# Single-bank PSUM tiles, a third row maximum in two half-width parts, and exponentials per 512 columns in a two-layer FNet and attention kernel

## The chip, the cores and the metric

The kernel runs on one core of a Trainium2 chip. A core has a matrix engine (TensorE, in the profile PE for matmuls and PEld for the loading of weights), a vector engine (DVE), a scalar engine (ACT), GpSimd (POOL) and a queue that issues most transfers (SP). Matmuls write to PSUM, a memory of eight banks of 512 float32 columns by 128 partitions; DVE and ACT read it. The metric is the device time in microseconds of one execution, and the median of several runs is reported.

## The reference, cut to what matters

```python
x = A_x                                            # 2048 x 512, float32
x = x + A(layernorm(x))                            # FNet
x = x + B(layernorm(x))                            # attention
x = x + A(layernorm(x))
x = x + B(layernorm(x))

def A(x):
    a = einsum("bsd,ed->bse", x, dft_hid_re)
    b = einsum("bsd,ed->bse", x, dft_hid_im)
    return einsum("ts,bse->bte", dft_seq_re, a) - einsum("ts,bse->bte", dft_seq_im, b)

def B(x):                                          # S = 2048, D = 512, 32 heads of 16
    q = (x @ wq).reshape(B, S, 32, 16).transpose(0, 2, 1, 3)
    k, v = x @ wk, x @ wv                          # one key and value head for all 32
    scores = einsum("bhqd,bkd->bhqk", q, k) * 16 ** -0.5
    o = einsum("bhqk,bkd->bhqd", softmax(scores), v)
    return o.transpose(0, 2, 1, 3).reshape(B, S, 512) @ wo
```

The softmax needs, for each of 2048 queries and 32 heads, the maximum of 2048 scores before the exponentials.

## The kernel before

Each of the two layers has a phase A (the FNet part, the layer normalisations, and the making of queries, keys and values) and a phase B (attention). The order of all instructions on each engine is written out by hand; the framework puts in the waits.

**PSUM.** The eight banks are given out under three names. `x` has two tiles of two banks each (`pair`, L68), `y` has three single banks and `z` one (`bank`, L65). A tile of a name is reused in turn, and a new use waits until the last reader of the whole tile is done. In phase A, `x` holds the sums of the sequence transform (`z_rows`, L854; two pairs make four accumulators) and of other products (`y_rows`, L632; `q_half`, L354; `q_rows`, L363). In phase B it holds the scores.

**Queries and keys.** A query tile `i` is 128 queries; there are NT = 16 of them per layer. `o.qT[i]` holds its 32 heads as 16 pairs `pr`; of a pair, one head lies in partitions 0 to 63 and one in 64 to 127 (`g` is 0 or 1). Queries and keys are split into high and low parts, which lie in 64 rows together, so a score matmul is 64 rows deep and occupies one row half of the matrix engine; two matmuls of different `g` can run side by side. `kz` holds the keys for both halves.

**The attention loop** (`phase_b`, L1213) runs over 16 x 32 steps, n = 32 i + s_. A step scores one block `c` of 128 keys against half of the heads of tile `i`: four matmuls `score` (L1031, matmul at L1048) of 512 columns, j = 0 to 3, with g = j mod 2. Two of them, one per row half, fill the two banks of an `x` tile, and one exponential of 1024 columns on ACT reads both (L1051) into a probabilities tile `ptiles` in `slot`. Two steps later `pv` (L1055, matmuls at L1062) multiplies the probabilities with the values: four matmuls, written as eight in the profile, 128 rows deep and 32 columns wide side by side, into the one bank of `z`. After 16 key blocks ACT and DVE copy the sum out (L1065, L1068).

**The maxima** for later query tiles are made in the same steps. A piece is 512 keys `kb` of one head: `max_half` (L555) calls `max_of` (L431), a matmul of 64 rows and 512 columns into a `y` bank (L434) and a `reduce_max` on DVE (L435) into the column `kb` of `o.mxp[i]`. `units` (L1000) lists all pieces of a layer in order, `more_max` takes the next one, and `share` (L1018) says whether a step makes two or three. The order in a step is score g, score 1-g, two maxima (one per half), score 2+g, score 3-g, third maximum. With three in a step the third stands alone, and the next step begins with the other half. When a tile's pieces are done, `max_neg_a` (L571) reduces its columns, and two steps later the negated maxima go by DMA into spare rows of `o.qT` (`max_rows`, L585), so that the score matmul subtracts them.

**Once per tile** the output of the tile before is projected at step 13 (`o_proj`, L1123, twelve full matmuls into a `y` bank, then an addition on DVE, L1129), and small statistics run on DVE for the next layer's normalisation (L1174 to L1189). In the last tile, when no maxima are left, the second score pair of a step uses two `y` banks and two exponentials of 512 columns (L1039 to L1044).

Of the kernel before, what the change touches and what calls it, by code (L numbers as in the profile page):

```python
# [17 lines left out]
P = 128  # L18
# [30 lines left out]
def fnet_mqa_kernel(ctx: ExitStack, tc: tile.TileContext, x_in, ct, dt_, wq, wkv, wo, out):  # L49
# [49 lines left out]
    eps = sb.tile([P, 1], F32, name="eps")  # L99
    nc.gpsimd.memset(eps, EPS)  # L100
    kone = sb.tile([P, 1], F32, name="kone")
    kmask = sb.tile([P, 1], F32, name="kmask")
    t_ = sb.tile([P, 1], F32, name="ktmp")
# [90 lines left out]

    class Layer:
        pass

    def make_layer(L, src, mid, dst, last):
# [4 lines left out]
        o.mxp = {}  # L203
        o.qT = {}
# [149 lines left out]
        def q_half(t0, g, xth, xtl, between=lambda: None):  # L354
            wh, wl = st["wqh", g]
            pq = pair()[:, 0, :256]
            for k in range(NK):
                ks = slice(k * P, (k + 1) * P)
                mm3(pq, wh[:, ks], wl[:, ks], xth[:, k, :], xtl[:, k, :], k == 0, k == NK - 1)
                between()  # L360
            q_split(t0, g, pq)

        def q_rows(t0, g0, xth, xtl, after):  # L363
            pq = pair()
            for h in range(2):
                for k in range(NK)[::1 - 2 * h]:
                    ks = slice(k * P, (k + 1) * P)
                    for u in (0, 1, 2)[::1 - 2 * h]:
                        for g in range(2):
# [3 lines left out]
                            nc.tensor.matmul(pq[:, g ^ h, :256], a[gs, ks], b[gs, k, :],  # L373
# [4 lines left out]
            for e in range(2):  # L378
                q_split(t0, g0 + e, pq[:, e, :256])
# [51 lines left out]
        def max_of(i, pr, g, c0, n, to, tag="y"):  # L431
            pm = bank(tag)[:, :n]
            gs = slice(64 * g, 64 * g + KR)
            nc.tensor.matmul(pm, o.qT[i][gs, pr, :], kz[gs, c0:c0 + n], start=True, stop=True)  # L434
            nc.vector.reduce_max(to, pm, axis=AX.X)  # L435

# [130 lines left out]
        def max_neg(i, p0=0, n=NPAIR, k=4):  # L567
# [3 lines left out]
        def max_neg_a(i, p0=0, n=NPAIR, k=4):  # L571
# [60 lines left out]
        def y_rows(tb, pairs, zh, zl, x1, after):  # L632
            ys = [pair() for _ in pairs]
            at = 0
            for h in range(2):
                for w, y in zip(pairs, ys):
                    for cc, k in [(c, k) for c in range(2) for k in range(NK)][::1 - 2 * h]:
                        for u in (0, 1, 2)[::1 - 2 * h]:
                            a, b = ((zh, dh), (zh, dl), (zl, dh))[u]
                            for g in order(0, 1):  # L640
                                gs = slice(64 * g, 64 * g + 64)
                                tt = w[g ^ h]
                                nc.tensor.matmul(y[:, g ^ h, :], a[cc][gs, k, tt * P:(tt + 1) * P], b[cc][gs, k, :],  # L643
# [8 lines left out]
                    else:  # L652
                        for e in range(2):
                            y_add(4 * tb + w[e], y[:, e, :], x1[w[e]])
# [128 lines left out]
        def phase_a(extra):  # L783
# [125 lines left out]
            for n in range(128):  # L909
# [7 lines left out]
                if s == 0:  # L917
                    za, zb = pair(), pair()
                    z = [za[:, 0, :], za[:, 1, :], zb[:, 0, :], zb[:, 1, :]]
# [69 lines left out]
            def rows_in():  # L989
# [10 lines left out]
        units = [(0, pr, g, 3) for pr in range(HALF, NPAIR) for g in range(2)]  # L1000
        units += [(i, pr, g, kb) for i in range(1, NT) for pr in range(NPAIR) for kb in range(4) for g in range(2)
                  if (i, pr, kb) not in early]
        o.done = 0

        def more_max():
            if o.done < len(units) and units[o.done][0] in o.loaded | {0}:
                max_half(*units[o.done])
                o.done += 1

        goals = []  # L1010
        for j in range(NT):
            for lim in (HALF, NPAIR):
# [3 lines left out]
                goals.append((sum(u[0] < j or (u[0] == j and u[1] < lim) for u in units), at))  # L1016

        def share(n):  # L1018
            slack = min([3 * (at - n) - (c - o.done) for c, at in goals if at > n], default=99)
            if slack >= SPARE:  # L1020
                st["light"] = True
            elif slack < 1:
                st["light"] = False
            return 2 if st.get("light") and n >= 4 else 3

        def done_with(i, pr):
            return all(u[:2] > (i, pr) for u in units[o.done:])
# [3 lines left out]
        def score(i, s_, j):  # L1031
# [6 lines left out]
            w = j // 2  # L1038
            if i == NT - 1 and jj == 1 and o.done == len(units):  # L1039
                e = bank("y")  # L1040
                nc.tensor.matmul(e, kz[64 * g:64 * g + KR, c * P:(c + 1) * P],  # L1041
                                 o.qT[i][64 * g:64 * g + KR, cp:cp + 4, :], start=True, stop=True)
                nc.scalar.activation(ptiles[i, s_][:, j, :], e, AF.Exp, scale=DH ** -0.5)
                return  # L1044
            first = "e" not in st
            if first:
                st["e"] = pair()
            nc.tensor.matmul(st["e"][:, g, :], kz[64 * g:64 * g + KR, c * P:(c + 1) * P],  # L1048
                             o.qT[i][64 * g:64 * g + KR, cp:cp + 4, :], start=True, stop=True)
            if not first:  # L1050
                nc.scalar.activation(ptiles[i, s_][:, 2 * w:2 * w + 2, :], st.pop("e"), AF.Exp, scale=DH ** -0.5)  # L1051
# [62 lines left out]
        def o_mm(k):  # L1114
            if k == 0:
                bt["po"] = bank("y")
# [11 lines left out]
        def o_add(i):  # L1128
            nc.vector.tensor_add(bt["x"], bt["po"], bt["x"])  # L1129
            (nc.sync if last else nc.gpsimd).dma_start(dst[i], bt["x"])  # L1130

        def finish():
# [3 lines left out]
            pt = bank("y")  # L1136
# [5 lines left out]
            rc = sb.tile([P, 4, 4], F32, name="rc")  # L1142
# [7 lines left out]
            pt = bank("y")[:, :256]  # L1150
# [62 lines left out]
        def phase_b(nxt):  # L1213
            nonlocal woh, wol, osp
            woh = slot(4, F32R).rearrange("p (k e) -> p k e", k=NK)
# [6 lines left out]
            for n in range(NT * NSTEP):  # L1222
# [48 lines left out]
            for at in behind:  # L1271
                pv(*at)
            return {**out_tasks(NT - 1), 12: [lambda: o_proj(NT - 1)]}
# [65 lines left out]
```

## Time and profile before

| What | us |
|---|---|
| median of 3 runs | 3532.45 |
| lowest and highest run | 3527.42, 3532.56 |
| span of the profiled execution | 3530.1 |
| PE, DVE, ACT, POOL busy in it | 3490.8, 2606.6, 2548.1, 877.0 |

The profile describes one execution, and its span is 2.35 us below the median of the runs. A row of the grouped view gives the line, the engine, the operation, output and input tiles and shapes, the count, then the busy time, the mean in ns of one, and the idle time of the engine before it with what ended that. A row of the timeline gives start and length in us from the start of the span, the engine, the line, the operation, how many of one kind are merged, and in brackets the idle time before it and what ended it. A row of the windows view gives a stretch, its length, the busy time and count of PE, PEld, DVE, ACT and POOL in it, the granted clock of the matrix engine, the share of the transfer engines and GB/s. PE's busy time counts a matmul from its start to its modelled end, and these overlap, so a busy share near 1 doesn't by itself say that PE is the limit.

### The profile page before, as it was taken

To read this page: it belongs to the slowest core of one execution; us is meant where nothing else is said; L and a number is where in the kernel's file an instruction comes from. 1 tells how busy PE (TensorE), PEld (TensorE's weight loads), DVE (VectorE), ACT (ScalarE), POOL (GpSimd) and SP (SyncE) were. 2 spreads that over 40 slices of the span, in tenths; PEclk is the share of its full clock that TensorE was granted. 3 is DMA by queue.
4 is the path that set the end of the run, shared out by engine and by line. 5 is a ranking of instruction groups with operands and counts; after the bars stand their busy time and mean duration, and the time that the engine had idled before them with its cause. 6 is when DMAs were issued, how large, how long until landed. Compare 5 with 4: busy or idle time off the path is not lost.

```text
span 3530.1 us, 64709 instructions
## 1 busy us (share of the span) xinstructions
PE 3490.8 (99%) x24576; PEld 1874.1 (53%) x24576; DVE 2606.6 (74%) x4903; ACT 2548.1 (72%) x3324; POOL 877.0 (25%) x1342
## 2 busy tenths in 40 slices
PE   8999999999999999999999999999999999999999
PEld 6887979433333333333378879883333333333333
DVE  6264756788888888888432747668888888888883
ACT  4325644888888888888932256549888888888888
POOL 4245452211221122112213454422101010111011
PEclk9999999999999999999999999999999999999999
DMA  6435242311111110111144352423111111011100
GB/s 189 151 143 185 85 156 85 91 50 35 36 39 48 32 26 23 50 35 26 40 138 124 127 160 103 140 70 93 44 35 35 50 35 38 23 35 38 37 24 25
DMA packets 225530, 255.62 MB, mean 72 GB/s; under 512 B 52896, under 2 KB 175040, under 8 KB 218052
## 3 DMA queue, kind: packets, MB, share of 16 engines
q1 hardware_dynamic: 210932, 234.04, 21.7%
q0 software_dynamic: 14144, 17.33, 1.6%
q8 instruction: 193, 3.16, 0.4%
q14 instruction: 117, 0.96, 0.1%
q10 hardware_dynamic: 144, 0.13, 0.0%
HBM read 187.69 MB, written 65.79 MB: 72 GB/s over the span
## 4 chain that ended last, share of the span: by engine, by line
PE 90%; issue 3%; POOL 2%; DVE 2%; ACT 2%; DMA 1%; SPq 0%; ACTq 0%; DVEq 0%; POOLq 0%
PE z L1062 29%; PE x L1048 19%; PE y L434 13%; PE x L863 10%; PE y L88 3%; PE y L89 3%; PE y L90 2%; PE y L523 2%; PE x L88 2%; PE x L90 2%; PE x L89 2%; PE z L523 1%; PE x L643 0%; DVE row L193 0%; PE y L1041 0%
## 5 line engine op out<-in xcount | busy, mean ns | idle before, releaser
L1051 ACT ACTIVATE slot<-x 128x1024 f32<-128x1024 f32 x2000 | 1946.5, 1025 | 276.7 <-PE x L1048 271.6
L435 DVE TENSOR_REDUCE mxp<-y 128x1 f32<-128x512 f32 x2912 | 1830.8, 684 | 190.7 <-PE y L434 178.2
L1062 PE MATMUL z<-slot,v 128*32 128x512 f32 x8192 | 1096.3, 605 | 1.6 <-DVE lnv L1186 0.7
L1048 PE MATMUL x<-slot,kz 64*128 64x512 f32 x2976 | 676.5, 450 | 1.9 <-ACT slot L1051 0.9
L1048 PEld LDWEIGHTS x<-slot,kz 64*128 64x128 f32 x2976 | 278.3, 183 | 746.0 <-ACT slot L1051 689.4
L434 PE MATMUL y<-kz,slot 64*128 64x512 f32 x2144 | 568.3, 395 | 0.4 <-DVE mxp L435 0.4
L1062 PEld LDWEIGHTS z<-slot,v 128*32 128x32 f32 x8192 | 163.4, 108 | 360.8 <-issue 329.7
L863 PE MATMUL x<-cl,xnh 64*128 64x512 f32 (+1 forms) x1536 | 352.1, 355 | 0.0
L863 PE MATMUL x<-ch,xnh 64*128 64x512 f32 (+1 forms) x1536 | 334.8, 359 | 7.1 <-ACT row L850 7.0
L863 PE MATMUL x<-ch,xnl 64*128 64x512 f32 (+1 forms) x1536 | 338.7, 359 | 0.2 <-ACT xnl L630 0.2
L434 PEld LDWEIGHTS y<-kz,slot 64*128 64x128 f32 x2144 | 270.7, 186 | 20.7 <-DVE mxp L435 8.2
L593 POOL DMA_DIRECT2D slot<-mt x224 | 111.7, 506 | 574.6 <-PE y L434 523.3
L1105 POOL TENSOR_TENSOR row<-row,row 128x256 f32<-128x256 f32 x63 | 47.1, 747 | 707.2 <-DMA row<-rd 683.7
L863 PEld LDWEIGHTS x<-ch,xnh 64*128 64x128 f32 x1536 | 202.9, 186 | 28.9 <-ACT row L850 9.6
L863 PEld LDWEIGHTS x<-cl,xnh 64*128 64x128 f32 x1536 | 210.9, 186 | 13.8
L863 PEld LDWEIGHTS x<-ch,xnl 64*128 64x128 f32 x1536 | 204.4, 186 | 20.8 <-issue 6.0
L79 ACT CAST ch<-craw 128x512 fp32r<-128x512 f32 x176 | 106.9, 627 | 125.3 <-PE x L90 87.1
L523 PE MATMUL y<-kz,slot 64*128 64x512 f32 x496 | 194.8, 400 | 0.4
L88 PE MATMUL x<-ch,xnh 128*128 128x512 f32 x384 | 154.2, 402 | 9.3 <-ACT ch L79 8.4
L80 POOL TENSOR_TENSOR cl<-craw,ch 128x512 fp32r<-128x512 f32 x96 | 122.2, 1294 | 135.2 <-ACT ch L79 118.0
L90 PE MATMUL x<-ch,xnl 128*128 128x512 f32 x384 | 153.1, 399 | 2.6 <-POOL xnl L709 2.6
L89 PE MATMUL x<-cl,xnh 128*128 128x512 f32 x384 | 152.7, 398 | 0.6 <-DVE cl L80 0.6
(216 smaller groups left out, 4474.5 us busy)
## 6 DMA issues: line engine op xcount, KB each, us to landing
craw<-ct_in SPq DMA_DIRECT2D x112, 512.0 KB
slot<-qd SPq DMA_DIRECT2D x44, 1024.0 KB
qd<-row SPq DMA_DIRECT2D x144, 128.0 KB
od<-row SPq DMA_DIRECT2D x252, 64.0 KB
row<-wqd SPq DMA_DIRECT2D x48, 256.0 KB
row<-x_in SPq DMA_DIRECT2D x32, 256.0 KB
mid<-row POOLq DMA_DIRECT2D x32, 256.0 KB, 2.4
craw<-ct_in SPq DMA_DIRECT2D x32, 256.0 KB
```

The costliest lines, as they stand in the source:

```text
L80: (eng or nc.vector).tensor_sub(lo, raw, f(hi))
L88: nc.tensor.matmul(ps_, ah, bh, start=start, stop=False)
L89: nc.tensor.matmul(ps_, ah, bl, start=False, stop=False)
L90: nc.tensor.matmul(ps_, al, bh, start=False, stop=stop)
L434: nc.tensor.matmul(pm, o.qT[i][gs, pr, :], kz[gs, c0:c0 + n], start=True, stop=True)
L435: nc.vector.reduce_max(to, pm, axis=AX.X)
L523: nc.tensor.matmul(pm, o.qT[i][gs, pr, :], k[gs, c0:c0 + 512], start=True, stop=True)
L593: (nc.gpsimd if r else nc.sync).dma_start(f(o.qT[i][row:row + 1, p0:p0 + n, 32 * a:32 * a + 32]), mt[32 * a + c:32 * a + c + n, 32 * b:32 ...
L863: nc.tensor.matmul(z[d], a[gs, s, d * P:(d + 1) * P], b[gs, :], start=first and q < 2 and e == 0, stop=last and q > 1 and e == len(turns) - 1)
L1048: nc.tensor.matmul(st["e"][:, g, :], kz[64 * g:64 * g + KR, c * P:(c + 1) * P], o.qT[i][64 * g:64 * g + KR, cp:cp + 4, :], start=True, sto ...
L1051: nc.scalar.activation(ptiles[i, s_][:, 2 * w:2 * w + 2, :], st.pop("e"), AF.Exp, scale=DH ** -0.5)
L1062: nc.tensor.matmul(a[32 * j:32 * j + 32, :], v1[:, c, :], pt[:, j, :], start=c == 0, stop=c == NT - 1)
```

## The change

All PSUM tiles become single banks: `x` has four, and `pair` gives a list of two. In phase B the banks are taken once per layer and passed round by hand: `o.x`, four for the scores, and `o.banks`, three for maxima, projection and the last tile. Each score has its own exponential of 512 columns. A step with three maxima makes two whole ones and, as the third, a part: 256 keys of one head in one row half and the same 256 keys of its partner in the other, side by side in one bank. One reduce gives both maxima. Between the two matmuls of a part, DVE copies one element from the first one's columns into the second one's, which makes the second wait for the first. The partial maxima have six columns for four: whole pieces use `kb`, parts use `kb` and `kb + 2` for the key blocks 2 and 3, and the unused ones hold -3.0e38. Which pieces are left is kept in `todo`, `parts` and `ahead`. Some small tiles are joined.

```diff
     def bank(tag):
-        return ps.tile([P, 512], F32, name=tag, bufs={"y": 3, "z": 1}[tag])
+        return ps.tile([P, 512], F32, name=tag, bufs={"x": 4, "y": 3, "z": 1}[tag])
 
     def pair():
-        return ps.tile([P, 2, 512], F32, name="x", bufs=2)
+        return [bank("x") for _ in range(2)]
...
-                o.mxp[i] = sb.tile([P, NPAIR, 2, 4 if i else 5], F32, name=f"mxp{i % 4}")
+                o.mxp[i] = sb.tile([P, NPAIR, 2, 6], F32, name=f"mxp{i % 4}")
+                nc.gpsimd.memset(o.mxp[i][:, :, :, 4:] if i else o.mxp[i][:, HALF:, :, 4:], -3.0e38)
...
-        def max_of(i, pr, g, c0, n, to, tag="y"):
-            pm = bank(tag)[:, :n]
+        def max_of(i, pr, g, c0, n, to):
+            pm = (o.banks.pop(0) if o.banks else bank("y"))[:, :n]
             gs = slice(64 * g, 64 * g + KR)
             nc.tensor.matmul(pm, o.qT[i][gs, pr, :], kz[gs, c0:c0 + n], start=True, stop=True)
             nc.vector.reduce_max(to, pm, axis=AX.X)
+            if o.banks:
+                o.banks.append(pm)
...
+        def whole(g):
+            u = next((u for u in ahead if g in u[3]), None)
+            if u is None:
+                if not todo or todo[0][0] not in o.loaded | {0}:
+                    return
+                u = (*todo.pop(0), {0, 1})
+                ahead.append(u)
+            i, pr, kb, gs = u
+            max_half(i, pr, g, kb)
+            if i + 1 < NT:
+                partial(i + 1)
+            gs.remove(g)
+            if not gs:
+                ahead.remove(u)
...
+        def part_next():
+            if parts:
+                return *parts.pop(), 1
+            for e, (i, pr, kb) in enumerate(todo):
+                if i in o.loaded | {0} and kb > 1:
+                    parts.append(todo.pop(e))
+                    return *parts[0], 0
+            return None
+
+        def part(at, g):
+            i, pr, kb, h = at
+            if g == 0:
+                st["pm"] = o.banks.pop(0)
+            pm = st["pm"]
+            gs, c0 = slice(64 * g, 64 * g + KR), 512 * kb + 256 * h
+            nc.tensor.matmul(pm[:, 256 * g:256 * g + 256], o.qT[i][gs, pr, :], kz[gs, c0:c0 + 256], start=True, stop=True)
+            if g == 0:
+                nc.vector.tensor_copy(pm[:1, 256:257], pm[:1, :1])
+                return
+            k = kb + 2 * h
+            nc.vector.reduce_max(partial(i)[:, pr, :, k], pm.rearrange("p (a n) -> p a n", a=2), axis=AX.X)
+            o.banks.append(pm)
...
-            if slack >= SPARE:
-                st["light"] = True
-            elif slack < 1:
-                st["light"] = False
-            return 2 if st.get("light") and n >= 4 else 3
+            slack = min([3 * (at - n) - left(j, lim) for j, lim, at in goals if at > n], default=99)
+            st["light"] = slack >= SPARE and not st.get("light") and n >= 4
+            return 2 if st["light"] else 3
...
-            first = "e" not in st
-            if first:
-                st["e"] = pair()
-            nc.tensor.matmul(st["e"][:, g, :], kz[64 * g:64 * g + KR, c * P:(c + 1) * P],
+            row = o.banks if i == NT - 1 and jj == 1 and not todo + parts + ahead else o.x
+            e = row.pop(0)
+            nc.tensor.matmul(e, kz[64 * g:64 * g + KR, c * P:(c + 1) * P],
                              o.qT[i][64 * g:64 * g + KR, cp:cp + 4, :], start=True, stop=True)
-            if not first:
-                nc.scalar.activation(ptiles[i, s_][:, 2 * w:2 * w + 2, :], st.pop("e"), AF.Exp, scale=DH ** -0.5)
+            nc.scalar.activation(ptiles[i, s_][:, j, :], e, AF.Exp, scale=DH ** -0.5)
+            row.append(e)
...
-                bt["po"] = bank("y")
+                bt["po"] = o.banks.pop(0) if o.banks else bank("y")
...
             nc.vector.tensor_add(bt["x"], bt["po"], bt["x"])
+            if o.banks:
+                o.banks.append(bt["po"])
...
+            o.x = pair() + pair()
+            o.banks = [bank("y") for _ in range(3)]
...
-                g = units[o.done][2] if o.done < len(units) else 1
-                left = share(n) if o.done < len(units) else 0
-                for j, m in ((g, 0), (1 - g, 2), (2 + g, 0), (3 - g, 2)):
-                    score(i, s_, j)
-                    for _ in range(m):
-                        if left:
+                n_max = share(n) if todo or parts or ahead else 0
+                at = part_next() if n_max == 3 else None
+                if at:
+                    for k, v in zip("asMssMsb", (0, 1, 0, 3, 0, 1, 2, 1)):
+                        if k == "s":
+                            score(i, s_, v)
+                        elif k == "M":
+                            whole(v)
+                        else:
+                            part(at, v)
+                else:
+                    g = side()
+                    for j, m in ((g, 0), (1 - g, min(n_max, 2)), (2 + g, 0), (3 - g, n_max - 2)):
+                        score(i, s_, j)
+                        for _ in range(m):
                             more_max()
-                            left -= 1
```

Below, a step's matmuls are named in the new order: a and b are the two matmuls of the part, M0 and M1 the two whole maxima (the number is the row half), and s1, s3, s0, s2 the scores by j. The order a, s1, M0, s3, s0, M1, s2, b alternates the halves 0 and 1.

More of the change, by code (lines that the diff above doesn't have):

```diff
@@ L203, in make_layer @@
         o.mxp = {}
+        o.banks = []
         o.qT = {}
@@ L355, in q_half @@
             wh, wl = st["wqh", g]
-            pq = pair()[:, 0, :256]
+            pq = bank("x")[:, :256]
             for k in range(NK):
@@ L917, in phase_a @@
                 if s == 0:
[L918 to L919 removed]
+                    z = pair() + pair()
                     if n == 112:
@@ L1135, in finish @@
             x_load(i)
-            pt = bank("y")
+            pt = o.banks.pop(0)
             for b in range(4):
@@ L1272, in phase_b @@
                 pv(*at)
+            if nxt is not None:
+                o.banks = []
             return {**out_tasks(NT - 1), 12: [lambda: o_proj(NT - 1)]}
```

51 lines of the change are left out of this document (22 added, 29 removed).

## The prediction

> **What bounds the kernel now.** First the page's top row, then the grouped instructions, then the two attention phases cut out by the windows view (they run from the first to the last weighted sum of each layer).
>
> ```profile
> PE 3490.8 (99%) x24576; PEld 1874.1 (53%) x24576; DVE 2606.6 (74%) x4903; ACT 2548.1 (72%) x3324; POOL 877.0 (25%) x1342
> L1051 ACT ACTIVATE slot<-x 128x1024 f32<-128x1024 f32 x2000 | 1946.5, 1025 | 276.7 <-PE x L1048 271.6
> L435 DVE TENSOR_REDUCE mxp<-y 128x1 f32<-128x512 f32 x2912 | 1830.8, 684 | 190.7 <-PE y L434 178.2
> 633.01:1768.00 1134.99, 1134.18 (x7759) 423.67 (x7758) 956.94 (x1686) 995.85 (x1080) 239.68 (x493) 1.00 0.14 40
> 2388.20:3519.60 1131.40, 1130.57 (x7757) 423.11 (x7756) 945.85 (x1597) 995.57 (x1080) 135.79 (x253) 1.00 0.14 39
> ```
>
> The two attention phases take 1135.0 and 1131.4 us, 64% of the span. PE is busy throughout at clock 1.00, but that column also counts a matmul that only waits for its pipeline, so the limit is sought in one step. L435 gives 2912/2 = 1456 maxima per layer. Four are made ahead, and the loop's `share` hands out the other 1452 as 476 steps of three, 12 of two and, at the end, 24 of none (476 x 3 + 12 x 2). So almost every step is the one below, from the timeline:
>
> ```profile
> 1214.31 1.89 DVE L435 TENSOR_REDUCE mxp<-y 128x1 f32<-128x512 f32 x3
> ...
> 1218.39 1.94 ACT L1051 ACTIVATE slot<-x 128x1024 f32<-128x1024 f32 x2 [0.20 <-PE x L1048]
> ...
> 1218.91 1.06 PE L1062 MATMUL z<-slot,v 128*32 128x512 f32 x8
> ...
> 1219.90 0.50 PE L1048 MATMUL x<-xnh,kz 64*128 64x512 f32 x2
> ...
> 1220.24 0.40 PE L434 MATMUL y<-kz,slot 64*128 64x512 f32 x2
> ...
> 1220.38 0.18 PEld L1048 LDWEIGHTS x<-xnh,kz 64*128 64x128 f32 x2 [0.18 <-ACT slot L1051]
> 1220.47 0.41 PE L1048 MATMUL x<-xnh,kz 64*128 64x512 f32 x2
> ...
> 1220.51 1.94 ACT L1051 ACTIVATE slot<-x 128x1024 f32<-128x1024 f32 x2 [0.18 <-PE x L1048]
> 1220.67 1.89 DVE L435 TENSOR_REDUCE mxp<-y 128x1 f32<-128x512 f32 x3 [0.23 <-PE y L434]
> 1220.72 0.38 PE L434 MATMUL y<-kz,slot 64*128 64x512 f32 x1
> ...
> 1221.03 1.07 PE L1062 MATMUL z<-slot,v 128*32 128x512 f32 x8
> ...
> 1227.04 1.89 DVE L435 TENSOR_REDUCE mxp<-y 128x1 f32<-128x512 f32 x3 [0.23 <-PE y L434]
> ```
>
> Six steps lie between 1214.31 and 1227.04: **2.122 us a step**. PE's starts add up to it: weighted sum 0.99, score pair 0.34 (its weights, 0.10, are exposed: 0.50 against 0.40), maximum pair 0.23, score pair 0.25, third maximum 0.31; together 2.12. The third maximum holds one row half for 0.23 while the other stands empty. DVE's three reduces start (1.89 - 0.68)/2 = 0.60 apart, so DVE needs 1.80 and is idle 0.32 between starts (the row's 0.23 counts to the reduce's end). ACT is the tighter neighbour: at 1220.38 PE's weights wait for an exponential.
>
> **The change, part by part.**
>
> (1) *Third maximum in halves.* The new order a, s1, M0, s3, s0, M1, s2, b gives either row half 256 + 3 x 512 columns, against 4 x 512. Do the halves run on when they are out of step? The late sequence stage shows it:
>
> ```profile
> 521.98 0.39 PE L523 MATMUL z<-kz,slot 64*128 64x512 f32 x1
> 521.99 0.27 PE L863 MATMUL x<-ch,xnl 64*128 64x256 f32 x1
> 522.10 0.39 PE L523 MATMUL y<-kz,slot 64*128 64x512 f32 x1
> 522.22 0.28 PE L863 MATMUL x<-ch,xnl 64*128 64x256 f32 x1
> 522.34 0.28 PE L863 MATMUL x<-ch,xnh 64*128 64x256 f32 x2
> ```
>
> A 512-column matmul holds its half 0.24 while the other half passes 256 columns in 0.11 and begins the next 512. So 256 columns cost 0.12, and PE saves 0.23 - 0.12 = 0.11: its own work falls to **2.01**.
>
> (2) *The copy on DVE* between a and b is in no row. Nearest rows, and the row that costs most:
>
> ```profile
> 1242.93 0.15 DVE L1186 TENSOR_SCALAR lnv<-mv 128x1 f32<-128x1 f32 x1
> 1243.12 0.15 DVE L1187 TENSOR_SCALAR lnw<-lnv 128x1 int32<-128x1 int32 x1
> 1243.18 1.28 DVE L435 TENSOR_REDUCE mxp<-y 128x1 f32<-128x512 f32 x2
> ```
>
> One element takes 0.15, but the reduce behind L1187 starts 0.06 later; L1187 itself starts 0.19 after L1186, whose result it needs. Bounds: 0.06 overlapped; 0.29 when drained on both sides (0.11 lost ahead, because the reduce before must end, 0.68 + 0.03 instead of 0.60, and 0.18 for itself). It cannot be below nothing: it is an added instruction. I take 0.07: its operands come from PE, not from a DVE result just made. DVE's work is then 1.87. Behind the copy in DVE's queue stands M0's reduce; it needs M0, which ends later than a, so it loses nothing. Behind b's wait on PE stands the next weighted sum. With a's end 0.38 after the step's first weights, copy 0.03 + 0.15 and weights 0.16, b could go at 0.72, and is due at 0.81.
>
> (3) *Four exponentials for two.* The last 24 steps already mix both sizes on a saturated ACT:
>
> ```profile
> 3509.80 1.23 ACT L1043 ACTIVATE slot<-y 128x512 f32<-128x512 f32 x2
> 3510.77 1.18 ACT L1051 ACTIVATE slot<-x 128x1024 f32<-128x1024 f32 x1
> 3511.70 1.24 ACT L1043 ACTIVATE slot<-y 128x512 f32<-128x512 f32 x2
> ```
> ```profile
> L527 ACT ACTIVATE kraw<-y 128x512 f32<-128x512 f32 x128 | 76.8, 600 | 13.9 <-PE y L523 9.1 <-DVE mxe L533 2.3 <-PE x L863 2.1
> ```
>
> Two of 512 take 0.97, one of 1024 takes 0.93: ACT's step goes from 1.86 to 1.94, still under 2.01. The steps without maxima pay outright: 48 x 0.04 = +2 us. Upper end: no overlap at all, four times the 0.60 that one such instruction lasts (L527), 2.4 a step; the tail speaks against it.
> The Trainium skill, page "ScalarE: Activation LUTs", section "What ACT_TABLE_LOAD costs", speaks against this split: a fixed 186 ns plus 0.833 ns a column, 93 ns of it overlapped, which makes an estimate of 0.52 for 512 columns and 2.08 a step. Here the tail's 0.485 disagrees, and the sum goes by the trace.
>
> (4) *What becomes late next.* By the engines alone the step would be PE's 2.01, but the waits close two rings. The bank list hands M1 the bank that the part of the step before has just used. From a part's reduce at B: it ends at +0.68, M1's weights follow 0.06 later and are exposed (0.10), M1 0.23, b 0.12, turn to the weighted sum 0.08 (0.31 - 0.23): +1.27. Next first weights 0.99 on, exposed weights 0.10 and a 0.12: M0 at +2.48. Its reduce 0.43 later (1220.24 to 1220.67): +2.91; the part's is two reduces on: **B + 4.11 after two steps, 2.06 each.** ACT's ring, from the end of the exponential of s2, whose bank the next s2 needs: 0.05 (1218.39 + 1.94 to 1220.38) + 0.10 + 0.23 + 0.08 + 0.99, s1 to its exponential 0.61 (1219.90 to 1220.51), 3 x 0.485 + 0.60: 4.11 again. The same sum for today's second pair (0.05 + 0.10 + 0.23 + 0.31 + 0.99 + 0.61 + 0.92 + 1.02 = 4.23, 2.12 each) fits what is measured. So a step is worth 2.122 - 2.06 = 0.062, and 2 x 476 of them **-59 us**.
>
> (5) *Disturbances now paid in full*, because a ring has no slack:
>
> ```profile
> 1231.38 0.50 PE L1048 MATMUL x<-xnh,kz 64*128 64x512 f32 x2
> ...
> 1231.54 0.69 DVE L1129 TENSOR_TENSOR row<-y,row 128x512 f32<-128x512 f32 x1 [2.62 <-issue]
> ...
> 1232.29 0.18 PEld L434 LDWEIGHTS y<-kz,slot 64*128 64x128 f32 x1 [0.38 <-DVE row L1129]
> ...
> 1273.25 1.07 PE L1062 MATMUL z<-slot,v 128*32 128x512 f32 x8
> ...
> 1274.24 0.50 PE L1048 MATMUL x<-xnl,kz 64*128 64x512 f32 x2
> ...
> 1274.58 0.38 ACT L1065 COPY row<-z 128x256 f32<-128x256 f32 x1
> ...
> 1274.99 0.42 DVE L1068 COPY row<-z 128x256 f32<-128x256 f32 x1 [0.21 <-ACT row L1065]
> ...
> 1275.34 1.88 DVE L435 TENSOR_REDUCE mxp<-y 128x1 f32<-128x512 f32 x3
> ...
> 1275.47 1.07 PE L1062 MATMUL z<-slot,v 128*32 128x512 f32 x8
> ```
>
> Every 16 steps DVE copies a finished sum: reduces start 1.10 after the first score instead of 0.77; today DVE's idle 0.32 hides part, and PE loses 0.10 in that step (1273.25 to 1275.47 is 2.22) and, I estimate, 0.08 in the next. After the change M0's reduce is due 0.65 after the first weights, while the exponentials hold ACT until about 0.48 (0.61 + 4 x 0.485 - 2.06); its copy ends at 0.86, and DVE's, 0.03 later, lets the reduce go after 0.35, at 1.24: 0.59 late. Extra 0.41 x 62 = **+25 us** (bounds: 0 if the slack stays, 37 if all 0.59 is new). The output projection's bank goes to M1 in mid-step instead of to the last maximum; M1 waits for L1129 to end 0.85 into its step and streams at 1.01 instead of 0.62; the rings, emptied by the projection, give about half of that back: 0.2 x 30 = **+6**. DVE's other small work (statistics, reciprocals, a maximum over 6 instead of 4 columns) had 0.32 to hide in and now has 0.19: some 0.3 a tile x 30 = **+8**, between 0 and 15.
>
> (6) *At nothing:* constants in one tile (setup only); POOL's fill of the new columns, a tile ahead of use on an engine 25% busy (uncovered: one late reduce per tile, under 10 us in all). No DMA is added or moved past another. Single banks instead of pairs in the sequence stage can only end stalls:
>
> ```profile
> PEld x L863 <- ACT row L850: 4.8, 4, 2.1
> ```
>
> That is the first layer; 0 taken, -10 for both the end.
>
> **Sum:** -59 + 25 + 6 + 8 + 2 = -18 on a span of 3530.1, thus 3512. The median of the runs, 3532.45, is 2.35 above that span (the runs: 3527.42 to 3532.56), so the forecast is **3514 us**.
>
> **Rivals.**
> *The rings stay open; PE binds.* If M1's and s2's weights go in before the bank is free (matmul alone waiting), both rings lose 0.10 and fall to 2.01. Then 952 x 0.11 = -105, with half of (5) and the tail +22: 3450; with a partial opening up to 3495. Against it: L434's weights at 1232.29 wait for DVE. Chance 0.17.
> *Slower: the copy is drained.* At 0.29, DVE's step is 1.80 + 0.29 + 0.08 of other work (the first window's 957 busy less 1452 x 0.63, over 512 steps) = 2.17: +0.048 x 952 = +46, 3578. It decides from 2.122 - 1.88 = 0.24 on. For it: L1187's 0.19. Against: it awaits PE, not DVE. Chance 0.20.
> *ACT binds.* At 0.53 per exponential (2.122/4) the gain is gone; at 0.52, ACT's step with L1065's share (0.3/16) is 2.10: 952 x 0.02 = -19 and tail +9, projection +6: 3528, no change. Against: 0.485 in the tail. Chance 0.08. The skill's estimate above would give this one.
> *The change does not do what it says:* b waits so long for the copy that the halves never overlap. PE keeps 2.01 plus that wait; it needs 0.11 for nothing to be gained, and (2) finds 0.09 to spare. Time 3530. Chance 0.05.
>
> **How the numbers follow.** Forecast 0.50, its own range 3496 (half of (5)) to 3534 (37 and 15 there). A measurement of this kernel tells about 0.2%, 7 us, from no change: faster is below 3525, slower above 3540. Faster: 0.40 of the forecast's half, 0.17 of the open rings: 0.57. Same: 0.10 of the forecast, 0.07 of ACT, 0.04 of the last: 0.21. Slower: the drained copy's 0.20 and 0.02 of the last two: 0.22. The range takes the drained copy's price in and leaves out what is dearer still and the widest opening of the rings, a tenth on either side: 3465 to 3578.
>
> **What the profile after would show.** Right: steps of about 2.06, longer at every sixteenth; nearly 476 parts a layer whose reduce writes 128x2; exponentials of 512 starting 0.48 apart; M1's weights waiting for DVE and s2's for ACT. Open rings: steps of 2.01 with neither wait. Drained copy: copies starting after the reduce before has ended, no idle DVE. Wrong altogether: a step above 2.12 with DVE and ACT both idle in it, or a weighted sum that waits for b.

## The result, and the profile after

The changed kernel takes **3512.39 us**, the median of four runs (3507.57 to 3514.82), against 3532.51 for the kernel before, timed beside it: a ratio of 0.9946, with a 95% interval of 0.9932 to 0.996. That is 20 us less; the forecast was 3514.

The page of the changed kernel: its top row and two of its groups (line, engine, operation, count | busy us, mean ns of one | idle time before, and what ended it).

```profile
PE 3460.8 (99%) x25536; PEld 1999.7 (57%) x25536; DVE 2690.7 (77%) x5863; ACT 2657.0 (76%) x5324; POOL 880.6 (25%) x1374
L436 DVE TENSOR_REDUCE mxp<-y 128x1 f32<-128x512 f32 x1952 | 1254.5, 684 | 58.7 <-PE y L435 6.6
L1047 DVE TENSOR_REDUCE mxp<-y 128x2 f32<-128x512 f32 x960 | 653.8, 681 | 1.0 <-PE y L1042 1.0
```

The third maxima are now the 960 reduces of L1047, 480 a layer, beside 1952 of L436, together the 2912 of before. PE's busy time fell by 30 us, the busy time of DVE and ACT rose by 84 and 109. The windows view over the same two attention phases, from the first to the last weighted sum of a layer, shows where the span got shorter:

```profile
633.61:1758.20 1124.59, 1116.76 (x8235) 489.80 (x8234) 998.47 (x2166) 1051.04 (x2077) 240.52 (x503) 1.00 0.14 40
2377.00:3499.40 1122.40, 1113.41 (x8234) 488.11 (x8233) 989.59 (x2075) 1049.29 (x2077) 136.76 (x263) 1.00 0.14 39
```

By the starts of the weighted sums the first phase fell by 9.9 us and the second by 9.0. What lies ahead of, between and behind them changed by -0.7 together. So all of the gain is in the attention steps, and the timeline of the changed kernel shows what a step is now:

```profile
1213.57 0.68 DVE L1047 TENSOR_REDUCE mxp<-y 128x2 f32<-128x512 f32 x1
...
1213.74 0.38 PE L1042 MATMUL y<-kz,slot 64*128 64x256 f32 x1
...
1214.17 0.14 DVE L1044 COPY y<-y 1x1 f32<-1x1 f32 x1
...
1214.31 0.18 PEld L435 LDWEIGHTS y<-kz,slot 64*128 64x128 f32 x1 [0.16 <-DVE y L1044]
1214.32 0.49 PE L435 MATMUL y<-kz,slot 64*128 64x512 f32 x1
...
1214.65 0.27 PE L1042 MATMUL y<-kz,slot 64*128 64x256 f32 x1
...
1214.85 1.07 PE L1096 MATMUL z<-slot,v 128*32 128x512 f32 x8
1215.60 0.68 DVE L1047 TENSOR_REDUCE mxp<-y 128x2 f32<-128x512 f32 x1
...
1216.42 0.42 PE L435 MATMUL y<-kz,slot 64*128 64x512 f32 x1
...
1217.70 0.68 DVE L1047 TENSOR_REDUCE mxp<-y 128x2 f32<-128x512 f32 x1
```

The part's reduces start 2.03 and 2.10 apart: two steps take 4.13, **2.065 each**, where the prediction's ring gave 4.11 and 2.06. The ring can be seen closing. The reduce of 1213.57 ends at 1214.25, and the weights of M1 start at 1214.31, the 0.06 of the prediction. (The row names the copy of L1044 as the releaser. But that copy ends only at 1214.31, as the weights start, and it is the reduce that frees the bank; the copy only came last in DVE's queue.) These weights are exposed, so M1 lasts 0.49; in the step behind it finds its bank free and lasts 0.42. So a long step and a short one take turns.

The steps that the prediction charged with 25 us are those in which a finished sum is copied. Here is one, with the end of the step ahead of it, in the changed kernel:

```profile
1266.63 1.06 PE L1096 MATMUL z<-slot,v 128*32 128x512 f32 x8
...
1267.62 0.38 PE L1042 MATMUL y<-kz,slot 64*128 64x256 f32 x1
...
1267.98 0.41 ACT L1099 COPY row<-z 128x256 f32<-128x256 f32 x1
...
1268.42 0.42 DVE L1102 COPY row<-z 128x256 f32<-128x256 f32 x1 [0.37 <-ACT row L1099]
1268.76 0.14 DVE L1044 COPY y<-y 1x1 f32<-1x1 f32 x1
1268.83 1.27 DVE L436 TENSOR_REDUCE mxp<-y 128x1 f32<-128x512 f32 x2
...
1268.96 0.38 PE L1042 MATMUL y<-kz,slot 64*128 64x256 f32 x1 [0.27 <-DVE y L1044]
...
1269.27 1.06 PE L1096 MATMUL z<-slot,v 128*32 128x512 f32 x8
```

From 1266.63 to 1269.27 this step takes 2.64. DVE's half of the sum's copy (L1102) waits for ACT's half (L1099), the one-element copy stands behind L1102 in DVE's queue, and b waits for that copy, with the weighted sum behind it. M0's reduce starts at 1268.83, 1.21 after the step's first weights, where 1.24 was expected.

### The profile page after: what moved, and what is told of

Its sections match the earlier page's. It is cut to its first block, busy times and chain, and to the rows that moved or that the text cites. A ratio compares the mean times of both kernels' runs of the same rounds, so it can differ in the third digit from the quotient of the medians.

```text
span 3510.5 us, 68668 instructions
## 1 busy us (share of the span) xinstructions
PE 3460.8 (99%) x25536; PEld 1999.7 (57%) x25536; DVE 2690.7 (77%) x5863; ACT 2657.0 (76%) x5324; POOL 880.6 (25%) x1374
## 4 chain that ended last, share of the span: by engine, by line
PE 83%; ACT 5%; DVE 4%; issue 4%; POOL 2%; DMA 1%; SPq 0%; ACTq 0%; DVEq 0%; POOLq 0%
PE z L1096 27%; PE x L1082 11%; PE x L866 11%; PE y L1042 9%; PE y L435 7%; ACT slot L1084 3%; PE y L88 3%; PE y L526 2%; PE y L89 2%; PE y L90 2%; PE x L88 2%; PE x L90 2%; PE x L89 2%; PE z L526 1%; DVE row L1102 1%
## 5 line engine op out<-in xcount | busy, mean ns | idle before, releaser
L1084 ACT ACTIVATE slot<-x 128x512 f32<-128x512 f32 x3992 | 2059.3, 612 | 148.4 <-PE x L1082 129.7
L436 DVE TENSOR_REDUCE mxp<-y 128x1 f32<-128x512 f32 x1952 | 1254.5, 684 | 58.7 <-PE y L435 6.6
L1082 PE MATMUL x<-slot,kz 64*128 64x512 f32 x2968 | 820.2, 428 | 0.3
L1047 DVE TENSOR_REDUCE mxp<-y 128x2 f32<-128x512 f32 x960 | 653.8, 681 | 1.0 <-PE y L1042 1.0
L1042 PEld LDWEIGHTS y<-kz,slot 64*128 64x128 f32 x1408 | 258.5, 184 | 613.5 <-DVE mxp L436 569.3
L1042 PE MATMUL y<-kz,slot 64*128 64x256 f32 x1408 | 475.9, 338 | 10.7 <-DVE y L1044 10.3
L1082 PEld LDWEIGHTS x<-slot,kz 64*128 64x128 f32 x2968 | 436.0, 184 | 61.8 <-issue 41.3
L435 PEld LDWEIGHTS y<-kz,slot 64*128 64x128 f32 x1440 | 263.6, 185 | 78.9 <-DVE y L1044 30.8
```

Of the source, the lines that this page charges most:

```text
L1042: nc.tensor.matmul(pm[:, 256 * g:256 * g + 256], o.qT[i][gs, pr, :], kz[gs, c0:c0 + 256], start=True, stop=True)
L1047: nc.vector.reduce_max(partial(i)[:, pr, :, k], pm.rearrange("p (a n) -> p a n", a=2), axis=AX.X)
```

## The experiments

Two questions were open. Is it the two rings that hold a step at 2.065, or an engine's own work, or the one-element copy? And is the loss of a sixteenth step (one in which a finished sum is copied) due to b or to the reduces? Ten kernels were run, each an edit of the changed kernel. Where three rounds or more were run, the ratio is to the kernel before, timed on the same chip (medians 3530.76, 3530.83 and 3529.71); e2, e4 and e5 have a single time.

**e1: exponentials alone, without parts.** Every step with three maxima takes the branch without a part.

```diff
-                at = part_next() if n_max == 3 else None
+                at = None
```

> The change without its parts: every step makes three whole maxima in the old order, and only the single banks and the exponentials of 512 columns stay. Rings (my theory): the step falls back to PE's own work, 2.12 us, and the time to that of the kernel before, 3525 to 3540 us, with 2 us more in the steps without maxima. Rival (the finer exponentials, which free score banks earlier, carry the gain, not the halved maximum): steps near 2.06 and a time near 3512 us.

Measured: 3524.7 us, ratio 0.9984 (0.9975 to 0.9994), just under the lower edge of what the rings gave. The timeline of its DVE, the first and the last of four steps' reduces:

```profile
1214.10 1.89 DVE L436 TENSOR_REDUCE mxp<-y 128x1 f32<-128x512 f32 x3 [0.24 <-PE y L435]
...
1220.46 1.89 DVE L436 TENSOR_REDUCE mxp<-y 128x1 f32<-128x512 f32 x3 [0.24 <-PE y L435]
```

Three steps take 6.36, 2.12 each, as before the change. Shorter exponentials with single banks, without the parts, are worth some 6 us; the rest of the gain needs the parts.

**e2: parts alone, with score tiles of two banks.** The exponentials go back to 1024 columns, which need both scores of a pair, so the order of the step is another one too.

```diff
+            o.x = [ps.tile([P, 2, 512], F32, name="x", bufs=2) for _ in range(2)]
...
-                    for k, v in zip("asMssMsb", (0, 1, 0, 3, 0, 1, 2, 1)):
+                    for k, v in zip("assMMssb", (0, 1, 0, 1, 0, 3, 2, 1)):
```

> The parts alone: scores in tiles of two banks again, one exponential of 1024 columns per pair, in the order a, s1, s0, M1, M0, s3, s2, b. Rings: PE's own work is still 2.01 us a step, but the second pair's bank comes free only at the end of the longer exponential, and both of its scores wait for it; added up over two steps this ring gives 2.18 us, so steps near 2.18 and a time of 3590 to 3630 us, slower than before. Rival (the halved maximum alone carries the gain, the exponentials' split is idle): steps of 2.06 or less and 3480 to 3515 us.

Measured: 3609.56 us. Its part's reduces, with one left out between:

```profile
1215.23 0.68 DVE L1048 TENSOR_REDUCE mxp<-y 128x2 f32<-128x512 f32 x1
...
1219.61 0.68 DVE L1048 TENSOR_REDUCE mxp<-y 128x2 f32<-128x512 f32 x1
```

Two steps take 4.38, 2.19 each: slower than before the change. With e1 this says that neither half of the change carries the gain by itself. Since the order changed along with the exponentials, e2 doesn't tell which of the two costs the 0.12 that a step is longer here than in the changed kernel.

**e3: the copy doubled.** A second element of the same bank is copied, and b waits for both.

```diff
                 nc.vector.tensor_copy(pm[:1, 256:257], pm[:1, :1])
+                nc.vector.tensor_copy(pm[:1, 257:258], pm[:1, 1:2])
```

> The changed kernel with a second one-element copy behind the first (another element of the same two columns). Rings: the copy stands in DVE's idle time outside the ring, so the steady step stays at 2.06 us; only the steps disturbed by other DVE work get longer, in all 3 to 20 us, 3515 to 3532 us. Rival (the copy is paid in every step, and its price is what keeps the gain from the 105 us that PE saves): 0.07 us more in each of 960 steps, 3575 to 3585 us.

Measured: 3589.43 us, ratio 1.0167 (1.015 to 1.0184). The expectation from the rings, 3515 to 3532, was missed; the rival's 3575 to 3585 came nearer, and e9 below tests its reason. The timeline:

```profile
1250.56 0.38 PE L1042 MATMUL y<-kz,slot 64*128 64x256 f32 x1
...
1250.98 0.15 DVE L1044 COPY y<-y 1x1 f32<-1x1 f32 x1
...
1251.17 0.15 DVE L1045 COPY y<-y 1x1 f32<-1x1 f32 x1
...
1251.38 0.18 PEld L1042 LDWEIGHTS y<-kz,slot 64*128 64x128 f32 x1 [0.15 <-DVE y L1045]
...
1251.69 0.16 PEld L1097 LDWEIGHTS z<-slot,v 128*32 128x32 f32 x8
```

The second copy starts only when the first has ended, 0.19 after its start, so b's weights go 0.82 after the step's first weights; with one copy that is 0.63. (The prediction's 0.72 for one copy is the time of b itself, with 0.10 for its exposed weights.) The weighted sum follows 0.31 later, at 1.13, and the next first weights 0.99 behind it. Here is a third ring, closed within one step: first weights, a, copy, b, weighted sum, first weights. It comes to 2.12, against 1.93 with one copy. That had some 0.13 to spare under a step of 2.065 (the prediction's 0.09 is what it has under PE's 2.01); the added 0.19 uses it up, and the steps are 2.13.

**e9: the copy doubled where nothing waits for it.** The second copy is of a constant, in a small tile outside PSUM that b has nothing to do with.

```diff
                 nc.vector.tensor_copy(pm[:1, 256:257], pm[:1, :1])
+                nc.vector.tensor_copy(t_[:1], kone[:1])
```

> A second one-element copy on DVE right behind the first, but of one constant into a row of its own, so that neither b nor the first copy has to do with it. It takes DVE's time alone. Rings (DVE's own work 1.87 + 0.07 is under 2.06; the first whole maximum's reduce starts at most 0.07 later in the ring): 3512 to 3545, by 0 to 0.035 us a step. Rival (the doubled copy's +77 us was the price of DVE's time): near 3590.

Measured: 3516.47 us, ratio 0.9962 (0.9948 to 0.9976), 4 us above the changed kernel (6 by the ratios, whose intervals overlap). Its DVE:

```profile
1249.27 0.15 DVE L1044 COPY y<-y 1x1 f32<-1x1 f32 x1
1249.34 0.14 DVE L1045 COPY ones<-ones 1x1 f32<-1x1 f32 x1
```

This copy starts 0.07 after the first and takes DVE's time alone. So the 77 us of e3 are not the price of one more instruction on DVE. Since the copy of e3 holds DVE longer (0.19), its own rows must say the rest: its first copy starts 0.04 after a's end, as in the changed kernel (0.05), so DVE isn't late for it, and what grew is the wait in the ring through b. The rival of the prediction that DVE becomes the bound falls too: 960 more instructions on it cost 4 us.
The Trainium skill, page "VectorE: DVE Perf Modes", section "The DRAIN you can't avoid", says that the next operation does not start until the pipe is empty, that one which is not held starts earlier, and that in eight copies a semaphore after each cost nothing extra. The 0.07 of e9 agrees with the second point; for these one-element copies the wait did cost something, 0.19 from start to start against 0.07.

**e4: DVE's work shortened.** All maxima leave out an eighth of their keys (448 of 512 columns), and the exponent's argument is a sixteenth; the instructions and waits stay.

```diff
-            nc.vector.reduce_max(to, pm, axis=AX.X)
+            nc.vector.reduce_max(to, pm[:, :n - 64], axis=AX.X)
...
-            nc.vector.reduce_max(partial(i)[:, pr, :, k], pm.rearrange("p (a n) -> p a n", a=2), axis=AX.X)
+            nc.vector.reduce_max(partial(i)[:, pr, :, k], pm.rearrange("p (a n) -> p a n", a=2)[:, :, :224], axis=AX.X)
...
-            nc.scalar.activation(ptiles[i, s_][:, j, :], e, AF.Exp, scale=DH ** -0.5)
+            nc.scalar.activation(ptiles[i, s_][:, j, :], e, AF.Exp, scale=DH ** -0.5 / 16)
```

> All maxima of the attention loop read 448 of the 512 columns (64 keys are left out), which takes 0.067 us from each reduce; the exponentials take a sixteenth of the argument, so that none overflows. Three reduces and the end of one lie in DVE's ring over two steps: it falls from 2.06 to about 1.97. Rings: ACT's ring, 2.05, takes over at once; steps of 2.05 us in place of 2.065, 10 to 20 us less in all (3490 to 3505), and the second whole maximum's weights wait no longer for DVE. Rival (DVE's ring alone holds the step): PE's own 2.01, some 45 us less. Rival (ACT's ring alone): no change at all, 3512.

Measured: 3482.12 us, below the rings' 3490 to 3505. Its part's reduces, the first and the last of eight steps, and M1 in one of them:

```profile
1241.39 0.62 DVE L1047 TENSOR_REDUCE mxp<-y 128x2 f32<-128x448 f32 x1
...
1250.44 0.39 PE L435 MATMUL y<-kz,slot 64*128 64x512 f32 x1
...
1257.73 0.62 DVE L1047 TENSOR_REDUCE mxp<-y 128x2 f32<-128x448 f32 x1
```

Eight steps take 16.34, 2.043 each. M1 is at 0.39, its weights no longer exposed, so DVE's ring is open. The step is still not at PE's 2.01: ACT's ring is right behind. With the 0.478 that lies between exponentials (below) its sum is 4.09 for two steps, 2.045 each. The traces show the two rings change places. In the changed kernel M1's weights wait for DVE in 880 steps and those of s2 for ACT in 68; here it is 30 and 848 (waits over 0.02 us counted). The gain was somewhat larger than expected: ACT's ring was taken 0.007 a step too long, which is some 7 us.

**e5: the part's bank returned out of turn.** It goes to M0 of the next step instead of M1.

```diff
-            o.banks.append(pm)
+            o.banks.insert(1, pm)
```

> The part's bank goes back to the front region of the list, so that the first whole maximum of the next step takes it, instead of the second. Nothing is computed otherwise. Rings: the ring now closes in one step: part's reduce 0.68, first whole maximum's weights 0.06 later and 0.10 exposed, 0.43 from it to its reduce, and two reduces on 1.20: 2.47 us a step, 952 steps, about 3890 us. Rival (the order of the banks does not matter, an engine's own work binds): 3512. Between, over 3600: the ring is there but one of its terms is smaller.

Measured: 3841.16 us. The timeline:

```profile
1214.53 0.68 DVE L1047 TENSOR_REDUCE mxp<-y 128x2 f32<-128x512 f32 x1
...
1215.26 0.18 PEld L435 LDWEIGHTS y<-kz,slot 64*128 64x128 f32 x1 [0.42 <-DVE y L1044]
...
1217.01 0.68 DVE L1047 TENSOR_REDUCE mxp<-y 128x2 f32<-128x512 f32 x1
```

The reduce ends at 1215.21, M0's weights start 0.05 later, and the next reduce of a part is 2.48 on, against 2.47 worked out. No instruction was added and none made longer, yet the kernel is 9% slower than the changed one. This is the strongest evidence for the ring through the banks. The total came out 49 us under the estimate: in a step of 2.48 the disturbances have room again, and the estimate had left them in at their full price. By the mean steps, a sixteenth step with its neighbours takes 2.48 each like the others, where the changed kernel loses some 0.55 (33 us in all), and the projection's two steps exceed ordinary ones by 0.6 less than there (18 us).

**e6: the sum copied by ACT alone.** The end of the kernel is left as it was.

```diff
-                nc.scalar.copy(oa[:, :256], a[:, :256])
...
-                ob = half(0)[:, :256] if end else oa[:, 256:]
-                nc.vector.tensor_copy(ob, a[:, 256:])
...
+                else:
+                    nc.scalar.copy(oa, a)
```

> The finished weighted sum is copied by ACT alone in one instruction of 512 columns (about 0.6 us); DVE copies nothing of it, except for the last tile's end. So the one-element copy and the reduces of a sixteenth step are not held up. Theory (the 64 long steps lose 0.55 each because DVE's half of the copy stands ahead of the one-element copy and the reduces): a long step falls from 2.64 to 2.3-2.45, the time to 3495-3502. Rival (ACT's ring pays instead: its exponentials start 0.2 later than now): long steps as before or longer, 3510-3520.

Measured: **3492.09 us**, ratio 0.989 (0.9875 to 0.9906): 20 us below the changed kernel, and below both expectations. The timeline of the step that ended at 1269.27 in the fence above:

```profile
1260.88 1.06 PE L1096 MATMUL z<-slot,v 128*32 128x512 f32 x8
...
1262.24 0.62 ACT L1105 COPY row<-z 128x512 f32<-128x512 f32 x1
...
1262.91 1.07 PE L1096 MATMUL z<-slot,v 128*32 128x512 f32 x8
...
1264.88 0.18 PEld L1082 LDWEIGHTS x<-xnl,kz 64*128 64x128 f32 x1 [0.22 <-ACT slot L1084]
...
1265.31 1.06 PE L1096 MATMUL z<-slot,v 128*32 128x512 f32 x8
```

The one-element copy has nothing of the sum ahead of it in its queue, and the step takes 2.03. The loss comes one step on, 2.40, through ACT's ring: there the weights of a score wait for an exponential. Four steps around it (one ahead, the copy's own and two behind) take 8.54 on the mean, against 8.88 in the changed kernel. By the starts of the weighted sums the two phases fell by 16 of the 20 us.
The Trainium skill, page "TensorEngine Tiling (Array Packing)", section "PSUM Bottleneck", advises to use both ScalarE and VectorE for PSUM evacuation. Here the two halves lie in one bank and run one behind the other, 0.41 and 0.42, and one instruction of 0.62 is the better choice.

**e10: the one-element copy first.** In a sixteenth step DVE's half of the sum's copy is emitted behind the one-element copy.

```diff
+                    st["sum"] = lambda: nc.vector.tensor_copy(ob, a[:, 256:])
...
                 nc.vector.tensor_copy(pm[:1, 256:257], pm[:1, :1])
+                st.pop("sum", int)()
```

> In a sixteenth step the one-element copy is queued on DVE ahead of DVE's half of the sum's copy, instead of behind it; nothing else moves. Theory A (the loss goes through b alone: PE waits in that step for the one-element copy): the long step falls by 0.3, 64 of them, about 3493 us. Theory B (as the prediction had it: the reduces behind the sum's copy are still 0.55 late, and the next step's second whole maximum waits for a bank): the loss moves one step on, 3505-3512.

Measured: 3507.09 us, ratio 0.9931 (0.9919 to 0.9944). The timeline:

```profile
1266.47 1.07 PE L1097 MATMUL z<-slot,v 128*32 128x512 f32 x8
...
1268.27 0.42 DVE L1106 COPY row<-z 128x256 f32<-128x256 f32 x1 [0.22 <-ACT row L1100]
...
1268.74 1.07 PE L1097 MATMUL z<-slot,v 128*32 128x512 f32 x8 [0.17 <-DVE row L1106]
...
1269.80 0.68 DVE L1048 TENSOR_REDUCE mxp<-y 128x2 f32<-128x512 f32 x1
...
1270.54 0.18 PEld L435 LDWEIGHTS y<-kz,slot 64*128 64x128 f32 x1 [0.30 <-DVE y L1044]
...
1271.08 1.07 PE L1097 MATMUL z<-slot,v 128*32 128x512 f32 x8
```

b no longer waits for the copy, and yet the step is 2.27. A wait that neither theory had shows here: `z` has one bank, and the weighted sum of 1268.74 stands idle for 0.17 until L1106 has read the finished sum out of it. M0's reduce, too, still stands behind L1106, and the part's reduce behind that ends at 1270.48; M1 of the next step gets its bank 0.06 later. That step takes 2.34. So theory A fails. Theory B has the time and the late bank right: most of the loss moves one step on, some 0.2 stays in the step through the bank of `z`, and only 0.1 goes.

**e11 and e12: no part in the sixteenth steps.** The planner's steps of two maxima, seven early in each layer, are put there instead; e11 with the changed kernel's copy of the sum, e12 with that of e6.

```diff
-            st["light"] = slack >= SPARE and not st.get("light") and n >= 4
+            st["light"] = slack >= SPARE and n >= 17 and n % NT == 1
```

> The sum's copy stays split between ACT and DVE; the steps of two whole maxima and no part are put at the sixteenth steps (30 a layer, as far as the plan's slack allows) instead of the 7 early ones, so no one-element copy and no third reduce stand behind DVE's half there. Rings (the loss of 0.55 is DVE's reduces coming late; without the part the next reduce of a part is a reduce earlier, so on time, and ACT's delay of about 0.3 remains): long steps and the ones behind them lose 0.2-0.35 in all, 3492-3502. Rival (ACT's part of the copy is what costs): 3508-3515.

Measured: 3507.06 us, ratio 0.9936 (0.9921 to 0.9951), outside the rings' expectation. The edit did not do all that it was to do: the planner's slack lasts for 7 of 30 such steps in each layer, the first seven. Where it was done, the timeline shows:

```profile
701.20 1.06 PE L1096 MATMUL z<-slot,v 128*32 128x512 f32 x8
...
702.99 0.42 DVE L1102 COPY row<-z 128x256 f32<-128x256 f32 x1 [0.36 <-ACT row L1099]
703.33 1.28 DVE L436 TENSOR_REDUCE mxp<-y 128x1 f32<-128x512 f32 x2
...
703.46 1.06 PE L1096 MATMUL z<-slot,v 128*32 128x512 f32 x8 [0.22 <-DVE row L1102]
```

The step takes 2.26 instead of 2.62 to 2.64, and by the next start (705.48) nothing comes behind it: 2.02. Fourteen such steps at some 0.37 are 5 us. An undisturbed step of two maxima took 1.96 in the changed kernel, 0.10 less than one of three, so moving them gives back 1.4 of that. The kernel is 5 us faster by the medians and 3.5 by the ratios, whose intervals overlap. With neither the one-element copy nor the third reduce behind L1102, then, about half of the loss goes for good; what stays in these rows is the bank of `z` again, for which the weighted sum waits 0.22.

> The same placing, with the weighted sum copied by ACT alone. If what is left of the loss there (about 0.3 in two steps) is ACT's ring, DVE's relief changes nothing: 3488-3495. If DVE's ring still had a share: 3478-3486.

Measured: 3495.29 us, ratio 0.9904 (0.9888 to 0.9921), at the upper edge of its first expectation, with an interval that overlaps that of e6 and a median 3 us above it. With ACT copying the sum, relieving DVE is worth nothing in the seven steps of a layer where it was done.

## Why the prediction was right

**(1) PE's own work.** The rows of M0 and of the part answer to it: b lasts 0.27 and the weighted sum follows 0.20 after its start, so the halves run on out of step, and the short steps take 2.02 to 2.03. Single steps of 2.01 stand between longer ones in e4 and e6. A run of steps held by PE alone was reached in no kernel, because e4 runs into ACT's ring first; so 2.01 as a mean stays an estimate.

**(2) The copy.** It lasts 0.14 to 0.15, starts 0.43 after the first weights and ends in time for b at 0.72. 0.07 of DVE's time was the right bound of the two: e9 adds as much again for 4 us. The 0.09 to spare ahead of b was right as well, and it was more of a danger than it was given: e3 overruns it, and the kernel is slower than before. The rival in which the copy is drained named the wrong resource. It priced a copy of 0.29 as DVE's work and came to 3578; e3's copies take about that much, and cost more, 3589, in the wait of b.

**(3) Four exponentials.** The end of the second layer, in the ACT timeline of the changed kernel:

```profile
3472.97 1.09 ACT L1084 ACTIVATE slot<-x 128x512 f32<-128x512 f32 x2
...
3478.71 1.22 ACT L1084 ACTIVATE slot<-x 128x512 f32<-128x512 f32 x2
```

From the start of the first row to that of the last there are twelve exponentials, two to a row: 5.74, so 0.478 each, where 0.485 was taken from two rows. The last tile of a layer grew from 62.5 to 63.2 us, 1.4 for both layers with the few ring steps in it, against 2 forecast for the end. The estimate of 0.52 from the figures of the Trainium skill (page "ScalarE: Activation LUTs", section "What ACT_TABLE_LOAD costs") doesn't hold here, and with it falls the rival that ACT binds.

**(4) The two rings.** The main term holds in size and place. Away from disturbed steps the mean step fell from 2.127 to 2.068 in the first layer and 2.072 in the second: over 952 steps -52 to -56, against -59. That it is the banks and not an engine is shown by e5, where only the bank's order changes, and e4, where shorter reduces open DVE's ring. Of the two rings of 4.11, DVE's is the one that binds (4.13 measured); ACT's, with 0.478, is 0.02 a step behind it, as e4 found.

**(5) The disturbances.** Sizes first, each from the mean steps of the inner tiles. The excess of a sixteenth step and the one behind it, over two ordinary steps, grew by 0.36 to 0.39: 60 of them make 22 to 23 us (25 forecast, with 62). The step with the projection and the next together didn't gain their two times 0.06: 3.5 us (6). Its path is the one given:

```profile
1224.96 0.38 PE L1042 MATMUL y<-kz,slot 64*128 64x256 f32 x1
...
1225.12 0.69 DVE L1163 TENSOR_TENSOR row<-y,row 128x512 f32<-128x512 f32 x1 [2.62 <-issue]
...
1225.87 0.18 PEld L435 LDWEIGHTS y<-kz,slot 64*128 64x128 f32 x1 [0.50 <-DVE y L1044]
```

L1163 ends at 1225.81, 0.85 into the step, and M1's weights follow. DVE's other work costs 0.32 a tile in the first layer's two steps with statistics and, in both layers, 0.13 a tile in four steps of its second half: 9 us (8). In e4, where DVE has more room, both are gone (0.01 and none), so DVE's time is the cause. With -54 for the steps and 1.4 for the tail this is about -18, as in the prediction; the two phases as a whole fell by 19.

One path was incomplete. The prediction took the loss of a sixteenth step to go through late reduces to the next step's M1, and held that a weighted sum which waits for b would show it altogether wrong. In 60 steps it does wait for b, with PE idle for 0.17 to 0.29, since the one-element copy stands behind L1102 in DVE's queue, and (2) had named only what is queued behind the copy, not what stands ahead of it. The size was still right, and e10 says why: with b set free, the bank of `z` and the late reduces take the loss over almost whole. All three waits start from the same late L1102, and the prediction had priced only the last of them; that its 0.41 came so near to the 0.36 to 0.39 is in part luck. In the other steps PE is never idle for the copy, as predicted.

**(6) At nothing.** What lies outside the attention phases gave -0.7 us, within the 0 to -10 of the prediction.

## What to carry to other kernels

Before a matmul is cut so that PE has less to do, follow each buffer from its last reader to its next writer and add up the loop: with three banks in turn the loop through DVE, not PE's own work, set the step, and the order in which banks are handed on was worth 329 us. A tiny instruction is priced by who waits for it, and by what stands ahead of it in its queue: a second one-element copy cost 4 us where nothing waited, and 77 where a matmul did. When slack is used up, look at the disturbances that hid in it: here moving one copy off DVE's queue (e6) gained as much again as the whole change.

## What the runs showed of the hardware

A DVE copy that had to wait for the copy ahead of it started 0.15 to 0.19 after that copy's start (e3, all 960); one that did not mostly started 0.07 after (e9). In the changed kernel DVE's half of the sum's copy began 0.03 after the end of ACT's half in 63 of 64 copies (1267.98 + 0.41 to 1268.42), although they take different columns. The Trainium skill, page "PSUM — Partial Sum Buffer", section "PSUM bank collisions raise a hardware error", says that two engines must not touch one bank in the same partitions at once, and that the compiler's scheduler puts a dependency between them; the rows agree, and a sum in two banks wasn't tried.
